# Narrower waits for reused memory, a later read of a guard flag, and a newly searched instruction order in a linear-attention and softmax-attention kernel

## The chip, the cores and the metric

The kernel runs on one core of one Trainium2 chip. The metric is device time in microseconds (us), the median of the fast runs. Every run told here was of the fast state. A profile gives the span from the first to the last instruction, which is 1.7 to 1.8 us shorter than the time of the same run.

Engines: PE is TensorE (PEld its weight loads), DVE is VectorE, ACT is ScalarE, POOL is GpSimd, SP is SyncE, which issues DMAs here.

## The reference

Two attention blocks over separate inputs of 2048 tokens, 512 features and 32 heads of 16, their outputs side by side. Block A is linear attention and is the smaller part. Block B is full softmax attention and bounds the kernel:

```python
scores = jnp.einsum("bhqd,bhkd->bhqk", q, k) * scale
p = _softmax(scores, axis=-1)
o = jnp.einsum("bhqk,bhkd->bhqd", p, v)
return (...o...).reshape(B, S, D) @ wo
```

## The kernel before

B's scores are cut into 2048 blocks of 128 keys by 512 queries. PE computes a block (QK) in PSUM, the memory that its matmuls write (`pS` in the profiles). Then one of two engines turns it into probabilities in an fp16 slot of 512 columns in the big tensor `MEM`:

- ACT, with a real exponential over two or three blocks at once (`128x1024`, `128x1536`);
- DVE, with one scale-and-add that builds the bits of an approximate exponential. POOL adds two shifted copies of it, so such a block needs three PV matmuls instead of one.

PE then multiplies the slot with V (PV). All other work (projections, block A, output matmuls) is interleaved.

A planner in the Python of the kernel decides the order. It simulates the engines with fixed durations and latencies, picks what goes next, and gives each engine a fixed in-order stream. Its choices are steered by `TABLE`, one row of eleven parameters per 20 us of planned time. The recording layer then works out the semaphore waits:

```python
def add(self, lane, fn, reads=(), writes=(), ...):
    for k in writes:
        if k in self.parts:
            writes = list(writes) + self.parts.pop(k)
    ...
    for r in writes:
        w = self.last_write.get(r)
        if w is not None: ... deps.add(w)
        for rd in self.readers.get(r, ()): deps.add(rd)
    ...
    for r in writes:
        self.last_write[r] = op
        self.readers[r] = []
```

`MEM` holds x (16 slots' worth) and the weights W (12 slots' worth) until the last projection; then those 28 slots open for blocks. `parts` tells which x or W keys lie under a slot:

```python
for i in range(P0):
    sch.parts[("PT", i)] = ([("xTb", t) for t in range(4 * (i % 4), 4 * (i % 4) + 4)] if i < W0 else
                            [("Wb", kd, g) for kd in range(2) for g in range(NGP)] + [("Wb", 2)])
```

The first writer of a slot thus becomes a writer of all the keys under it, and the first writer of the next slot with the same keys waits for it, though the two slots share no address.

The approximation holds for a limited range of scores, so a flag computed on the chip guards it. Every engine reads the flag into a register and, at its end, branches to a slow general path if it is too large. The read stands 200 recorded operations after the flag's own:

```python
def emit_queue(self, queue, eng, sems, dma_inc=16, hook=None):
    for op in self.queue_ops[queue]:
        for d in op.waits: ... eng.wait_ge(sems[d.lane], val)
        if hook is not None and op.idx > hook[0]:
            hook[1](eng)        # wait for the flag, load it
            hook = None
        ins = op.fn(eng)
...
    sch.emit_queue(queue, e, sems, hook=(flag_op.idx + 200, hook))
    with e.If(got[0] > THRESHOLD_BITS): ...general path...
```

## Time and profile before

| | before |
|---|---|
| time, first 3 runs | 696.84 us (693.53 to 696.85) |
| span of the profile | 693.2 us |
| busy: ACT, PE, DVE, POOL | 97%, 95%, 83%, 56% |
| ACT: exponentials of two and three blocks, block A's | 518, 127, 32 |

The view to trust is ACT's start-to-start intervals. Records of consecutive ACT instructions overlap, so gaps of a few tenths of a microsecond vanish inside the "busy" share. From here on, ACT's own work is 0.904 us per exponential of two blocks, 1.331 of three, 0.477 of one (the medians of those intervals in the trace, which the prediction rounded to 0.905, 1.33 and 0.48). Whatever an interval has beyond that is called a stall. Every span below is then head (to the first exponential) + work + stalls + tail (from the end of the last exponential).

### The profile page before, as it was taken

Reading aid. Unit: us, or ns where it says so; the run is one execution under the profiler, and the core shown is the slowest. Engines: PE = TensorE matmul, PEld = TensorE weight load, DVE = VectorE, ACT = ScalarE, POOL = GpSimd, SP = SyncE. Lnnn points to the kernel's source line nnn. Section 1 sums busy time; section 2 is a strip of 40 time slices with the busy share of each in tenths; the row PEclk is TensorE's granted clock in tenths of the full one; section 3 lists DMA queues with packets and bytes.
Section 4 is the critical chain, followed back from the end, with each engine's and each line's share of the span. In section 5 each row is a group of like instructions: output and inputs, shape, how many; then the busy total and the mean of one; then the engine's idle time right before and its main releaser. Section 6 shows DMA issues by size and latency. Waiting matters only on the chain.

```text
span 693.2 us, 16233 instructions
## 1 busy us (share of the span) xinstructions
PE 661.5 (95%) x6619; PEld 220.0 (32%) x6673; DVE 576.8 (83%) x952; ACT 669.0 (97%) x683; POOL 390.4 (56%) x666
## 2 busy tenths in 40 slices
PE   8999999999999999999999999999889999999997
PEld 5323333333433333233223222333222222222222
DVE  5988889778778978788889888787888988888893
ACT  5999999999999999999999999999999999999995
POOL 5667656434254755544466667334456775667672
PEclk9999999999999999999999999999999999999999
DMA  9910000000000000000200100001000011000001
GB/s 212 234 43 1 1 2 4 10 11 11 2 1 1 2 1 1 10 9 10 42 21 2 25 17 24 9 9 39 17 25 1 17 24 43 20 17 17 1 32 35
DMA packets 36576, 17.36 MB, mean 25 GB/s; under 512 B 27536, under 2 KB 35984, under 8 KB 36496
## 3 DMA queue, kind: packets, MB, share of 16 engines
q1 hardware_dynamic: 35408, 15.61, 9.5%
q8 instruction: 54, 0.88, 0.5%
q10 hardware_dynamic: 1088, 0.66, 0.4%
q14 instruction: 26, 0.21, 0.1%
HBM read 4.46 MB, written 4.19 MB: 12 GB/s over the span
## 4 chain that ended last, share of the span: by engine, by line
PE 41%; ACT 38%; DVE 17%; issue 2%; DMA 1%; POOL 0%; DVEq 0%; ACTq 0%; POOLq 0%
ACT MEM L1001 37%; PE pS L786 15%; PE pPV L1130 13%; DVE MEM L887 10%; PE pS L655 3%; PE pS L549 2%; PE pS L734 2%; PE pS L624 1%; ACT EA L646 1%; DVE OT L1154 1%; DVE OT L1162 1%; DMA MEM<-in_B_x_dram 1%; PE pPV L1352 1%; DVE VV L633 1%; PE pS L583 1%
## 5 line engine op out<-in xcount | busy, mean ns | idle before, releaser
L1001 ACT ACTIVATE MEM<-pS 128x1024 f16<-128x1024 f32 (+1 forms) x645 | 656.5, 1202 | 10.7 <-PE pS L786 7.9
L1076 POOL INT64_ADD MEM<-MEM x639 | 382.7, 612 | 289.3 <-DVE MEM L887 250.3
L887 DVE TENSOR_SCALAR MEM<-pS 128x512 int16<-128x512 f32 (+1 forms) x590 | 403.7, 720 | 76.5 <-PE pS L786 72.5
L786 PE MATMUL pS<-QT,KM 32*128 32x512 bf16 x2048 | 271.9, 385 | 15.8 <-ACT MEM L1001 8.1
L1130 PE MATMUL pPV<-MEM,VV 128*17 128x512 f16 x3310 | 284.6, 382 | 1.0 <-DVE OT L1154 0.6
L786 PEld LDWEIGHTS pS<-QT,KM 32*128 32x128 bf16 x2048 | 71.6, 91 | 244.6 <-ACT MEM L1001 186.5
L1130 PEld LDWEIGHTS pPV<-MEM,VV 128*17 128x17 bf16 x3310 | 60.9, 88 | 121.9 <-issue 97.2
L655 PE MATMUL pS<-Wa,xTa 128*128 128x256 bf16 x256 | 39.3, 275 | 0.2 <-DVE MEM L887 0.2
L549 PE MATMUL pS<-MEM 128*128 128x512 bf16 x98 | 29.5, 383 | 3.0 <-issue 1.2
L1154 DVE STREAM_TRANSPOSE OT<-pPV 128x512 f32<-128x512 f32 x32 | 22.6, 706 | 7.1 <-PE pPV L1130 7.1
L655 PEld LDWEIGHTS pS<-Wa,xTa 128*128 128x128 bf16 x256 | 19.7, 97 | 17.9 <-issue 9.3
L527 DVE CAST KNa<-pS 128x512 bf16<-128x512 f32 x30 | 20.5, 684 | 3.2 <-PE pS L734 1.9
L646 ACT ACTIVATE EA<-pS 128x512 bf16<-128x512 f32 x32 | 22.3, 696 | 0.0
L624 PE MATMUL pS<-MEM 128*128 128x128 bf16 x256 | 19.8, 220 | 1.0 <-DVE MEM L887 0.5
L1162 DVE TENSOR_TENSOR OT<-OT,ZR 128x256 bf16<-128x256 f32 x32 | 18.1, 566 | 0.9
L1352 PE MATMUL pPV<-ZW 128*17 128x256 bf16 x101 | 18.2, 274 | 0.0
L624 PEld LDWEIGHTS pS<-MEM 128*128 128x128 bf16 x256 | 14.5, 98 | 9.2 <-issue 5.1
L734 PE MATMUL pS<-WOa,KNa 128*128 128x512 bf16 x51 | 15.8, 383 | 1.7 <-DVE MEM L887 0.9
L681 PE MATMUL pS<-xTa,Wa 128*128 128x512 bf16 x52 | 15.8, 383 | 1.3 <-issue 1.0
L549 PEld LDWEIGHTS pS<-MEM 128*128 128x128 bf16 x120 | 8.7, 97 | 20.1 <-issue 10.1
L647 DVE TENSOR_SCALAR EA<-EA 128x512 bf16<-128x512 bf16 x32 | 12.8, 401 | 2.3 <-ACT EA L646 2.1
L629 DVE CAST VV<-pS 128x512 bf16<-128x512 f32 x16 | 11.0, 686 | 2.9 <-PE pS L624 2.8
(80 smaller groups left out, 225.3 us busy)
## 6 DMA issues: line engine op xcount, KB each, us to landing
out_dram<-KNa SPq DMA_DIRECT2D x30, 128.0 KB, 1.7
Wa<-in_A_wqkv_dram SPq DMA_DIRECT2D x1, 1536.0 KB, 7.6
KM<-KR SPq DMA_DIRECT2D x96, 16.0 KB, 1.8
MEM<-in_B_wqkv_dram SPq DMA_DIRECT2D x2, 384.0 KB, 6.2
MEM<-in_B_wqkv_dram SPq DMA_DIRECT2D x1, 512.0 KB, 4.4
WOb<-in_B_wo_dram SPq DMA_DIRECT2D x1, 512.0 KB, 8.5
WOa<-in_A_wo_dram SPq DMA_DIRECT2D x1, 512.0 KB, 9.2
MEM<-in_B_x_dram ACTq DMA_DIRECT2D x1, 256.0 KB, 2.9
```

Of the source, the lines that this page charges most:

```text
L549: return e.matmul(f32v(bk), lhsT=Wb[:, cc, kind * 512 + Gp * 128:kind * 512 + Gp * 128 + 128], rhs=xTb[:, cc, sc * 512:(sc + 1) * 512], st ...
L624: return e.matmul(f32v(bk)[:, tl * 128:(tl + 1) * 128], lhsT=xTb[:, cc, t * 128:(t + 1) * 128], rhs=Wb[:, cc, 1024 + Gp * 128:1024 + Gp * ...
L646: ("act", 0.06 + n * 0.000833, f_ev("act", lambda e, bk: e.activation(EA[:, q, 0:n], f32v(bk)[:, c0:c0 + n], ACTF.Exp), [], [("EA", q)])),
L655: return e.matmul(f32v(bk)[:, 256 * tt:256 * tt + 256], lhsT=xTa[:, cc, (t2 + tt) * 128:(t2 + tt + 1) * 128], rhs=Wa[:, cc, 512 * kind + 2 ...
L734: return e.matmul(f32v(bk), lhsT=src, rhs=WO[:, hb, :], start=(hb == 0), stop=(hb == 3))
L786: return e.matmul(dst, lhsT=KM[32 * g:32 * g + 32, Gp % 2, e_, j * 128:(j + 1) * 128], rhs=QT[32 * g:32 * g + 32, Gp % 2, c * 512:(c + 1) ...
L887: sch.add("dve", lambda e: e.tensor_scalar(PTi[:, i * 512:(i + n) * 512], PS[:, b0 * 512:(b0 + n) * 512], ESC, EB, op0=ALU.mult, op1=ALU.add),
L1001: sch.add("act", lambda e: e.activation(PT[:, p0 * 512:p0 * 512 + w], PS[:, use[0] * 512:use[0] * 512 + w], ACTF.Exp, scale=SC), reads=[(" ...
L1076: sch.add("pool", lambda e: e.int64_add(PTl[:, pos * 128:pos * 128 + w], PTl[:, p0 * 128:p0 * 128 + w], v_), reads=[("PT", p0 + i) for i i ...
L1130: sch.add("pe", lambda e, g=g, j=j, hl=hl, pi=pi, k=k, first=first, last_=last_: e.matmul(PVb[32 * g:32 * g + 17, 0:512], lhsT=VV[:, Gp % ...
L1154: sch.add("dve", lambda e: e.transpose(OT[:, 0, :], PVb[:, 0:512]), reads=[("PV", g) for g in range(4)], writes=[("OT", 0)])
L1352: ins = e.matmul(dst, lhsT=ZW[:, 0:17], rhs=ZW[:], start=first, stop=first, tile_position=(0, 32 * g))
```

## The change

Three parts. A slot's first writer waits only for readers and writer of the memory under it and no longer becomes that memory's writer. The flag is read after everything else on each engine. And the order is new: `TABLE` comes from a beam search (a search that keeps only the best few tables at each step), and the planner counts 0.11 us between dependent DVE instructions (0 before) and 6.3 us instead of 5.0 for spreading K by DMA.

```diff
     def add(self, lane, fn, reads=(), writes=(), name="", queue=None,
             extra_deps=(), accum=None, force_signal=False):
-        for k in writes:
-            if k in self.parts:
-                writes = list(writes) + self.parts.pop(k)
...
+        for k in writes:
+            for r in self.parts.pop(k, ()):
+                deps.update(self.readers.get(r, ()))
+                if r in self.last_write:
+                    deps.add(self.last_write[r])
         for r in writes:
             w = self.last_write.get(r)
...
     TABLE = [      # 36 rows before, 33 after; almost all differ
-        (3, 0.05, 0.6, 1.0, 6, 9, 2, 0.8, 0.5, 4.0, 4),
+        (3, 0.1, 1.0, 0, 16, 8, 2, 0.8, 0, 4.0, 4),
...
-               ("dve", "dve"): 0.0, ("dve", "dma"): 0.12, ...
+               ("dve", "dve"): 0.11, ("dve", "dma"): 0.12, ...
...
-            st.append(("dma", 5.0, spread))
+            st.append(("dma", 6.3, spread))
...
-                              bank=False, ready=t_, prio=0.5))
+                              bank=False, ready=t_ + LAT["dve", "dve"], prio=0.5))
...
-            sch.emit_queue(queue, e, sems, hook=(flag_op.idx + 200, hook))
+            sch.emit_queue(queue, e, sems, hook=(len(sch.ops), hook))
```

## The prediction

> **What bounds the kernel now.** I read the busy shares first, then the chain that ended last, then ACT's own groups and its timeline.
>
> ```profile
> PE 661.5 (95%) x6619; PEld 220.0 (32%) x6673; DVE 576.8 (83%) x952; ACT 669.0 (97%) x683; POOL 390.4 (56%) x666
> ...
> PE 41%; ACT 38%; DVE 17%; issue 2%; DMA 1%; POOL 0%; DVEq 0%; ACTq 0%; POOLq 0%
> ```
>
> ACT is busy 669.0 of 693.2 us. The chain passes back and forth between ACT and PE, so these two wait for each other closely; PE's 95% says less, because matmul ends are modelled. Next, what one ACT instruction takes out of ACT's time. Mean durations (1119 and 1541 ns) overlap, so I take start to next start from the timeline (start, length, instruction, count):
>
> ```profile
> 505.14 9.27 ACT L1001 ACTIVATE MEM<-pS 128x1024 f16<-128x1024 f32 x10 [1.45 <-POOL MEM L1076]
> 514.20 0.70 ACT L646 ACTIVATE EA<-pS 128x512 bf16<-128x512 f32 x1
> 514.68 8.47 ACT L1001 ACTIVATE MEM<-pS 128x1024 f16<-128x1024 f32 x9
> ```
>
> Ten exponentials of two blocks run from 505.14 to 514.20: 0.905 us each. The one of 512 columns takes 514.68 - 514.20 = 0.48. So 512 columns cost 0.425, and three blocks 0.905 + 0.425 = 1.33 us. The counts come from the groups by shape:
>
> ```profile
> L1001 ACT ACTIVATE MEM<-pS 128x1024 f16<-128x1024 f32 x518 | 505.8, 1119 | 6.5 <-PE pS L786 3.9 <-POOL MEM L1076 1.8
> ...
> L1001 ACT ACTIVATE MEM<-pS 128x1536 f16<-128x1536 f32 x127 | 193.0, 1541 | 4.2 <-PE pS L786 4.0
> ...
> L646 ACT ACTIVATE EA<-pS 128x512 bf16<-128x512 f32 x32 | 22.3, 696 | 0.0
> ```
>
> ACT's unavoidable work is 518 x 0.905 + 127 x 1.33 + 32 x 0.48 = 468.8 + 168.9 + 15.4 = 653.1 us. The first exponential starts at 10.48 and the last ends at 684.20 (682.53 + 1.67 in the chain), 673.7 us apart. So 20.6 us of ACT's time between them are stalls, most of them hidden in the "busy" figure because each is shorter than the overlap of two records. Before lie 10.5 us of head, after it 9.0 us of tail (last PV, transposes, output matmuls, store). Head 10.5 + work 653.1 + stalls 20.6 + tail 9.0 = 693.2.
>
> Where are the stalls? I subtracted 0.905, 1.33 or 0.48 from every start-to-start interval on ACT. Two places stand out as the change's targets. The first is the moment when the memory of x and W opens for block slots:
>
> ```profile
> 497.38 1.99 ACT L1001 ACTIVATE MEM<-pS 128x1024 f16<-128x1024 f32 x2
> 500.17 2.14 ACT L1001 ACTIVATE MEM<-pS 128x1024 f16<-128x1024 f32 x2 [0.80 <-PE pS L786]
> 502.67 1.02 ACT L1001 ACTIVATE MEM<-pS 128x1024 f16<-128x1024 f32 x1 [0.36 <-POOL MEM L1076]
> 505.14 2.85 ACT L1001 ACTIVATE MEM<-pS 128x1024 f16<-128x1024 f32 x3 [1.45 <-POOL MEM L1076]
> ```
>
> Five exponentials took 505.14 - 497.38 = 7.76 us instead of 4.53: 3.2 us lost, and the releaser is POOL, which never otherwise holds ACT. The second is the read of the guard's flag in mid-stream:
>
> ```profile
> 283.81 1.02 ACT L1001 ACTIVATE MEM<-pS 128x1024 f16<-128x1024 f32 x1
> 285.86 2.36 ACT L1001 ACTIVATE MEM<-pS 128x1536 f16<-128x1536 f32 x2 [1.03 <-PE pS L786]
> ```
>
> 2.05 - 0.905 = 1.1 us lost. The sequencer records there show a register load of 0.47 us on ACT at 285.21, one of 0.49 on PE at 284.27, 0.54 on DVE and 0.50 on POOL, each followed by an ALU step and an assertion, 0.65 to 0.76 us per engine in all. One more stall of 1.7 us ends at 27.70 (early projections). The remaining 14.6 us are some fifty gaps of 0.1 to 0.9 us, nearly all released by the QK matmuls of PE.
>
> **What the Trainium skill says.** "ScalarE: Activation LUTs", section "What ACT_TABLE_LOAD costs", gives 0.833 ns per column for any function, and 186 ns less a 93 ns overlap as the fixed part. The slope agrees (0.425 us per 512 columns is 0.830 ns); the fixed part here is 0.905 - 0.853 = 0.05 us, so I use the trace. "DMA: Bandwidth & Descriptors", section "Latency and other measured facts", puts the floor of a register load at about 600 ns; here 0.47 to 0.54. "Runtime: NRT & Kernel Launch", section "Instruction fetch mechanics", says that a taken branch out of the fetched window stalls for a fetch. That seems to set the end here: ACT's closing branch at 689.76 is followed by its drain at 692.87, 3.1 us later, while POOL had seen the last store at 691.74.
>
> **The change part by part.**
>
> *Slot waits.* Before, the first writer of each of the 28 slots became a writer of all the x or W keys under it. The 12 slots of W therefore wait for one another in a single chain, the 16 of x in four chains, across ACT, DVE and POOL, though their addresses differ. After it, each waits only for readers (old projections, long done). This should remove the 3.2 us. I count 2.7: a little of the stall at 500.17 ended with PE and may be there anyway.
>
> *Flag read.* It leaves the middle: -1.1 on ACT. It is added at each engine's end, where ACT's path (last store issue, load, branch, fetch, drain) sets the finish: +0.7. POOL's read also comes after its wait for the last store: 691.74 + 0.76 plus its drain, still ahead of ACT's. Net -0.4.
>
> *Order.* This is the large part, and only the instruction counts are known:
> - exponentials of two blocks 518 to 534, of three 127 to 110: 19 blocks of 2048 move from ACT to DVE. ACT: 16 x 0.905 - 17 x 1.33 = 14.5 - 22.6 = -8.1 us.
> - DVE: 512-wide block instructions 549 to 594, 1024-wide 41 to 28. Start to start they take 0.60 and 1.13 in the trace: 45 x 0.60 - 13 x 1.13 = +12.3 us. DVE's busy time becomes 589, some 86% of the new span.
> - POOL: pairs of shifted copies 623 to 646, singles 16 to 8: 23 x 0.60 - 8 x 0.40 = +10.6 us, 59% of the span. No bound.
> - PE: 38 more PV matmuls, but 50 fewer zero filler matmuls (139 to 89; about 0.11 us apart in the trace, 5.5 us). With each run of matmuls priced at the quick end of what the same run took before, PE's stream sums to 634 us before and 629 after, an estimate. PE gets no heavier.
>
> The planner's added 0.11 us for a dependent DVE step and 6.3 instead of 5.0 us for the K copies cost nothing themselves; they make the plan's order more honest.
>
> Sum on ACT: -8.1 - 2.7 - 0.4 = -11.2. With the 16 us of other stalls taken as unchanged, the span goes from 693.2 to 682.0. Another -0.5 is a guess for fewer planned gaps: the fall in fillers says that the plan leaves PE idle less often. So 681.5 for the span, 11.7 less. From the median of 696.84 that gives 685.1; I say 685.0.
>
> **Rivals.**
> 1. *PE becomes the bound and gives ACT's gain back as stalls.* For it: most small stalls of ACT already end with QK. PE has 693.2 - 634 = 59 us not needed, and would keep 681.5 - 629 = 52; utilisation between the ends rises only from about 94% to 95%. If a third of the 8.1 comes back as QK-released gaps, the span is 684 and the time 688. I think this the likeliest way to miss.
> 2. *DVE becomes the bound.* In stretches without projections it is busy about 19 of 20 us already. More DVE blocks there would delay the freeing of the PSUM banks in which PE places the next blocks, so PE and then ACT wait. Against it: DVE was idle 116 us, mostly in stretches with other work. If half the added 12.3 us were exposed, there would be nearly no gain: 691.
> 3. *The opening wait is replaced.* Slots now free at once, but PV must still drain the POOL copies; if that is what limits, ACT loses the same 3 us slightly later: 688.
> 4. *The search also removes unplanned stalls.* If the 16 us fall by 5: 680.
>
> **Range and chances.** The arithmetic of -8.1 is firm, the 3.8 of removed waits nearly so; the uncertainty is how much of the residual 16 us grows or shrinks, to me a standard error of about 4.5 us, and the spread of the three times before (693.5 to 696.9) adds about 1. Range 678.5 to 691. Faster by over 2% means under 682.9, 2.1 us below my centre: 0.33. Slower by over 2% needs a blunder of 25 us: 0.01. The rest, 0.66.
>
> **What would show it.** ACT's count must be 534 and 110 and its stall total about 16 us instead of 20.6. Around the opening (after some 1490 of 2048 QK blocks) no interval on ACT may be released by POOL; if one is, the slot part is wrong. No register load stands in mid-stream; the interval from ACT's last store to its drain should grow from 3.1 to about 3.8 us. If ACT's intervals released by QK sum to well over 16 us, rival 1 or 2 holds; DVE's share of the releases of PE's weight loads tells which. The prediction would be badly wrong if the tail after the last exponential grew beyond 10 us, or if new waits on the K copies appeared on PE.

## The result, and the profile after

The changed kernel took 675.47 us (674.94 to 677.03, 4 runs), the kernel before 695.18 us (693.12 to 696.85, 4 runs): a ratio of 0.9722, 95% interval 0.9683 to 0.976. Ratios here are the mean time of one kernel's fast runs over that of the other's of the same rounds, so not quite the ratio of the quoted medians. The forecast of 685.0 with a range of 678.5 to 691.0 was too slow.

The page of the changed kernel, its busy shares and the chain that ended last:

```profile
PE 644.0 (96%) x6606; PEld 211.1 (31%) x6661; DVE 583.7 (87%) x984; ACT 658.1 (98%) x682; POOL 401.4 (60%) x681
...
ACT 74%; PE 17%; DVE 5%; issue 1%; DMA 1%; POOL 1%; ACTq 0%; DVEq 0%
```

The chain had lain on PE for 41% and on ACT for 38%. Now it runs along ACT for 74% of the span: ACT is seldom made to wait. Its groups by shape (busy us, mean ns, idle before):

```profile
L1000 ACT ACTIVATE MEM<-pS 128x1024 f16<-128x1024 f32 x534 | 520.2, 1172 | 0.7 <-PE pS L785 0.4
...
L1000 ACT ACTIVATE MEM<-pS 128x1536 f16<-128x1536 f32 x110 | 171.1, 1580 | 1.0 <-PE pS L785 1.0
```

The counts are those forecast. Visible idle time before them fell from 6.5 + 4.2 to 0.7 + 1.0 us. The mean duration of a two-block exponential rose from 1119 to 1172 ns although the work is the same. That is a good sign here: start to start they stay 0.904 us apart, and an exponential that had to wait has a shorter record (1.02 us in the single rows further below), so a longer mean says that fewer had to wait.

Where the 19.6 us between the two profiles come from:

| us | span | head | ACT work | stalls | tail |
|---|---|---|---|---|---|
| before | 693.2 | 10.5 | 652.6 | 21.1 | 9.0 |
| after | 673.6 | 8.8 | 644.4 | 10.7 | 9.7 |
| difference | -19.6 | -1.7 | -8.2 | -10.4 | +0.7 |
| predicted | -11.7 | 0 | -8.1 | -4.3 | +0.7 |

Work and tail came as forecast. The stalls fell 6.1 us further, and the head was 1.7 us shorter, which nobody had forecast.

The head can be settled from the traces. PE's first 20 projection matmuls, before and after (start, length):

```profile
6.33 3.57 PE L1232 MATMUL pS<-MEM 128*128 128x128 bf16 x20 [0.97 <-DMA MEM<-in_B_x_dram]
```

```profile
6.49 1.92 PE L1231 MATMUL pS<-MEM 128*128 128x128 bf16 x20 [1.53 <-DMA MEM<-in_B_x_dram]
```

The same matmuls take 3.57 or 1.92 us, and nothing in the change touches them. Either the change does this by some roundabout way, or the pace varies from run to run. The runs below decide.

### The profile page after: what moved, and what is told of

It reads as the page before. It is cut to its first block, busy times and chain, and to the rows that moved or that the text cites. A ratio compares the mean times of both kernels' runs of the same rounds, so it can differ in the third digit from the quotient of the medians.

```text
span 673.6 us, 16251 instructions
## 1 busy us (share of the span) xinstructions
PE 644.0 (96%) x6606; PEld 211.1 (31%) x6661; DVE 583.7 (87%) x984; ACT 658.1 (98%) x682; POOL 401.4 (60%) x681
## 4 chain that ended last, share of the span: by engine, by line
ACT 74%; PE 17%; DVE 5%; issue 1%; DMA 1%; POOL 1%; ACTq 0%; DVEq 0%
ACT MEM L1000 72%; PE pPV L1129 7%; PE pS L785 6%; DVE MEM L886 3%; ACT EA L645 2%; PE pS L548 1%; DMA MEM<-in_B_x_dram 1%; PE pS L654 1%; POOL MEM L1075 1%; DVE EA L646 1%; PE pS L680 0%; PE pS L1181 0%; DVE OT L1161 0%; DVE OT L1153 0%; PE pS L592 0%
## 5 line engine op out<-in xcount | busy, mean ns | idle before, releaser
L1000 ACT ACTIVATE MEM<-pS 128x1024 f16<-128x1024 f32 (+1 forms) x644 | 646.6, 1242 | 1.7 <-PE pS L785 1.4
L1075 POOL INT64_ADD MEM<-MEM x654 | 393.7, 615 | 258.2 <-DVE MEM L886 229.7
L886 DVE TENSOR_SCALAR MEM<-pS 128x512 int16<-128x512 f32 (+1 forms) x622 | 416.1, 706 | 53.1 <-PE pS L785 49.5
L1129 PE MATMUL pPV<-MEM,VV 128*17 128x512 f16 x3348 | 279.7, 382 | 0.6 <-DVE ZR L1160 0.3
L785 PE MATMUL pS<-QT,KM 32*128 32x512 bf16 x2048 | 264.1, 384 | 13.6 <-ACT MEM L1000 7.9
L785 PEld LDWEIGHTS pS<-QT,KM 32*128 32x128 bf16 x2048 | 68.9, 91 | 244.5 <-ACT MEM L1000 202.9
L1351 PE MATMUL pPV<-ZW 128*17 128x256 bf16 x75 | 14.5, 274 | 0.0
L548 PEld LDWEIGHTS pS<-MEM 128*128 128x128 bf16 x120 | 8.2, 97 | 18.5 <-issue 10.1
L733 PE MATMUL pS<-WOb,MEM 128*128 128x512 bf16 x40 | 12.4, 384 | 0.6 <-issue 0.6
```

The lines of the kernel that those rows point to most:

```text
L548: return e.matmul(f32v(bk), lhsT=Wb[:, cc, kind * 512 + Gp * 128:kind * 512 + Gp * 128 + 128], rhs=xTb[:, cc, sc * 512:(sc + 1) * 512], st ...
L733: return e.matmul(f32v(bk), lhsT=src, rhs=WO[:, hb, :], start=(hb == 0), stop=(hb == 3))
L785: return e.matmul(dst, lhsT=KM[32 * g:32 * g + 32, Gp % 2, e_, j * 128:(j + 1) * 128], rhs=QT[32 * g:32 * g + 32, Gp % 2, c * 512:(c + 1) ...
L886: sch.add("dve", lambda e: e.tensor_scalar(PTi[:, i * 512:(i + n) * 512], PS[:, b0 * 512:(b0 + n) * 512], ESC, EB, op0=ALU.mult, op1=ALU.add),
L1000: sch.add("act", lambda e: e.activation(PT[:, p0 * 512:p0 * 512 + w], PS[:, use[0] * 512:use[0] * 512 + w], ACTF.Exp, scale=SC), reads=[(" ...
L1075: sch.add("pool", lambda e: e.int64_add(PTl[:, pos * 128:pos * 128 + w], PTl[:, p0 * 128:p0 * 128 + w], v_), reads=[("PT", p0 + i) for i i ...
```

## The experiments

There were twelve runs. The first eight take the parts apart: each of the three alone, each pair, the kernel before again, and the old table with the new latencies. All instruction orders come from the two plans except where said. The new table with the old latencies could not be run: in simulation the order that it gives reads PSUM in the middle of an accumulation. So "the order" below is always the new table and the new latencies together.

In the table "stalls" are ACT's, worked out as above from each run's own profile.

| run | time | ratio to before | span | head | work | stalls | tail |
|---|---|---|---|---|---|---|---|
| before again | 696.13 | 0.9992 | 695.0 | 8.4 | 652.6 | 25.0 | 9.1 |
| slots | 690.66 | 0.9927 | 688.7 | 8.8 | 652.6 | 18.3 | 9.0 |
| flag | 697.21 | 1.0017 | 694.2 | 8.5 | 652.6 | 23.0 | 10.2 |
| slots + flag | 690.94 | 0.9939 | 689.2 | 8.6 | 652.6 | 17.8 | 10.2 |
| order | 679.15 | 0.9755 | 676.3 | 8.4 | 644.4 | 13.5 | 9.9 |
| order + slots | 674.55 | 0.9703 | 673.1 | 8.5 | 644.4 | 11.4 | 8.9 |
| order + flag | 678.05 | 0.9753 | 677.0 | 8.3 | 644.4 | 14.2 | 10.2 |
| all three, again | 675.07 | 0.9693 | 673.1 | 8.3 | 644.4 | 10.7 | 9.7 |
| old table, new latencies | 700.09 | 1.0071 | 697.5 | 8.5 | 666.9 | 11.9 | 10.2 |

### Before again: the head

No edit.

> The kernel before, once more, for the head: theory H says that the first 20 projection matmuls of PE take either about 1.9 or about 3.6 us from run to run in one and the same program (before's profile had the slow ones, after's the fast ones), so the 1.7 us of the head are no effect of the change. If they take 3.6 us again here and 1.9 in the three kernels with a changed part, something in the program causes it.

```profile
6.08 1.92 PE L1232 MATMUL pS<-MEM 128*128 128x128 bf16 x20 [1.36 <-DMA MEM<-in_B_x_dram]
```

The unchanged kernel now has the fast matmuls and a head of 8.4 us. So the 1.7 us are no effect of the change. A later run with the new order, the one with the rearranged end, had 3.57 us again. "TensorE: Matmul & The Clock Gate" of the Trainium skill, section "What's actually happening", describes a clock gate that halves the clock until PE has been busy for a window of some 3.4 us, and that window runs freely, so where it falls varies from run to run. A factor of 1.86 between 3.57 and 1.92 fits it, and the traces' own clock records agree: the first record of full clock starts at 10.47 and 9.69 us in the two profiles with the slow matmuls, and between 3.9 and 6.4 us in the other twelve (`--windows` shows 1.00 for the time ahead of that record).

The repeat brought a surprise as well. Its stalls are 25.0 us instead of 21.1, all of the difference in one place.

### The slot rule alone

```diff
 # before, with the change's rule in add(): nothing else
+        for k in writes:
+            for r in self.parts.pop(k, ()):
+                deps.update(self.readers.get(r, ())) ...
```

> Slot rule only, in the old order and with the old flag read. The program's instructions stay in the same order; only waits go. Theory S: 2.5 to 3.5 us off (about 692 us), the interval at the opening shrinks from 7.8 to about 5 us for five exponentials, no release by POOL there, and the small gaps elsewhere stay about 16 us. Theory K: 6 us or more off, with smaller gaps all through the last 190 us.

The result is 5.1 us by the ratio (0.9927, interval 0.9908 to 0.9946), between the two theories. At the opening ACT's stalls over 0.3 us are all gone in this run (none from 492 to 592 us), and with them the release by POOL. The opening in the repeat of the kernel before, on ACT's timeline:

```profile
498.10 2.14 ACT L1001 ACTIVATE MEM<-pS 128x1024 f16<-128x1024 f32 x2 [0.80 <-PE pS L786]
500.60 1.02 ACT L1001 ACTIVATE MEM<-pS 128x1024 f16<-128x1024 f32 x1 [0.36 <-POOL MEM L1076]
503.07 4.69 ACT L1001 ACTIVATE MEM<-pS 128x1024 f16<-128x1024 f32 x5 [1.45 <-POOL MEM L1076]
508.56 1.02 ACT L1001 ACTIVATE MEM<-pS 128x1024 f16<-128x1024 f32 x1 [0.80 <-PE pS L786]
510.18 2.10 ACT L1001 ACTIVATE MEM<-pS 128x1024 f16<-128x1024 f32 x2 [0.60 <-PE pS L786]
512.74 1.02 ACT L1001 ACTIVATE MEM<-pS 128x1024 f16<-128x1024 f32 x1 [0.47 <-PE pS L786]
514.36 1.02 ACT L1001 ACTIVATE MEM<-pS 128x1024 f16<-128x1024 f32 x1 [0.59 <-PE pS L786]
```

The first three rows are the waits seen in the first profile, to within 0.01 us. The four after them are new: PE is late, four times, for 0.5 to 1.0 us. The stretches of the same runs tell why. The columns after the length are the busy times of PE, PEld, DVE, ACT and POOL, then PE's granted clock. First the repeat of before, then the run with the slot rule:

```profile
490.00:505.00 15.00, 11.80 (x130) 3.68 (x129) 11.19 (x18) 12.14 (x13) 8.45 (x14) 1.00 0.11 27
505.00:512.00 7.00, 6.90 (x35) 1.32 (x32) 4.02 (x6) 5.55 (x7) 2.39 (x4) 0.55 0.15 37
512.00:516.00 4.00, 3.53 (x14) 0.80 (x14) 2.48 (x5) 2.57 (x4) 1.20 (x2) 0.51 0.00 0
```

```profile
490.00:505.00 15.00, 14.42 (x153) 4.87 (x155) 12.92 (x20) 14.83 (x16) 9.61 (x16) 1.00 0.11 27
505.00:512.00 7.00, 6.75 (x71) 1.95 (x68) 6.78 (x13) 7.00 (x10) 3.52 (x6) 1.00 0.15 37
512.00:516.00 4.00, 4.00 (x56) 0.89 (x48) 4.00 (x8) 4.00 (x6) 3.10 (x7) 1.00 0.02 4
```

In the repeat PE pauses behind the slot waits, and then its clock is granted at half (0.55, 0.51 in these stretches; by the trace's clock records from 505.65 to 515.89 us). PE gets through 35 matmuls in seven microseconds instead of 71. In the first profile of the kernel before, the same stretch had a clock of 1.00 and no such stalls. So the slot waits cost 3.2 us in each of the three profiles with the old order and the old rule, and more where the clock falls behind them: 3.5 us in the repeat, 2.4 in the run with the flag alone, nothing in the first profile. The skill's page, in the same section, has the clock fall to a half after at least one idle window of about 3.4 us. The half agrees; the idling does not. In the 3.41 us before the fall PE was busy for 1.87 us, and its longest pause was 1.54 us. A pause of 1.55 us stands in the first profile too, with no fall behind it. What decides between the two, no run shows.

The run-to-run spread carries the same mark. Over the 90 fast runs of the kernel before whose clock is on record, time and mean granted clock correlate at -0.88: 14 runs at a clock of 0.998 or more have a mean of 693.5 us, 19 runs from 0.990 to under 0.993 one of 698.0. The 16 runs with the slot rule average a clock of 0.9987 and a median of 690.66. They are not wholly free of it: two of them, at 0.995, took 694.5 and 695.4 us.

Theory K had the wrong reach (nothing lasts to the end of the kernel) but the right kind: a wait can have a sequel, through the clock and not through the order of streams.

### The flag alone

```diff
-            sch.emit_queue(queue, e, sems, hook=(flag_op.idx + 200, hook))
+            sch.emit_queue(queue, e, sems, hook=(len(sch.ops), hook))
```

> Flag read at each engine's end only, old order, old slot rule. Theory S: -1.1 in mid-stream, +0.7 at the end, so within 0.1% of before. Theory K: 2 us or more off, since the gaps of 0.9 us some 13 us after the old flag read and others like it go as well.

The ratio is 1.0017 (0.9995 to 1.004): nothing, or a little worse. ACT's stall at the old place fell from 1.14 to 0.49 us and not to zero. The gap of 0.95 us thirteen microseconds later stayed, so it was no sequel of the flag. The tail grew from 9.1 to 10.2 us, more than the 0.7 forecast. The load and its checks take 0.6 us on ACT as expected, and besides the last store's issue on ACT took 1.34 us instead of 0.37 to 0.41. In every profile with the flag at the end it took 0.92 to 1.40 us; why, no run shows.

### The order alone, and the pairs

```diff
 # the change's TABLE, the three LAT, spread and ready lines; old add(), old hook
```

> New order only: the new table and planner latencies; the old rule for block slots and the old mid-stream flag read stay. Theory S (sum of independent parts): the order alone carries most of the gain, time 679 to 682 us, ACT stalls after the first exponential about 14 to 15 us (10.7 as in the full change, plus about 3 at the opening of the slots and about 1 at the flag). Theory K (knock-on: in-order engines stay out of step long after a wrongly placed wait, so waits and order multiply): 684 us or more, and ACT's small gaps after the opening are larger than in the full change.

Measured 679.15 us with stalls of 13.5 us: theory S. The opening is cheaper in this order. It costs 0.68, 0.36 and 1.16 us on ACT, 2.2 in all, with a release by POOL again.

> The full change without the flag part: new order, new slot rule, flag still read in mid-stream (at another place of the new order). Theory S (independent parts; flag worth nothing): within 0.1% of the full change, about 675 to 676 us; ACT stalls about 11.3 us with one near the flag read of some 0.6 us, tail 9.0 instead of 9.7 us.

> The full change without the slot part. In the order-only run the opening cost 2.2 us on ACT, in the old order 3.2 to 6.7. If the slot rule's worth depends on the order, this should be 677 to 679 us, 2 to 3 us above the full change and not 5; if it were worth the same 5 us in every order, 680 us or more.

> Both wait parts in the old order: slots alone gave -5 us and the flag alone 0 to +1, so 690 to 692 us, ACT stalls about 17.5 us. The distance from here to the full change is then the order alone with clean waits: -8.2 of ACT work and about -7 of stalls, 15 us. In particular the gaps near 25.7 (1.7 us), 174 (0.6), 296 (0.95) and 401 (0.7) must still be there, as in every run of the old order, if they belong to the order; if they came from the old waits or the flag they are gone.

Order + slots took 674.55 us, against 675.47 and 675.07 for all three: the flag part gains nothing and may cost up to 1 us. Order + flag took 678.05, 2.6 to 3.0 us over all three, as expected. But its profile has a stretch at half clock too, from 381.46 to 384.87 us, far from the opening and with no pause of PE over 0.34 us in the 3.41 us before; it cost ACT 1.26 us. The other pair, order against order + slots, gives 4.6 us (3.6 by the ratios to before). So the slot rule's worth in the new order lies between 2.6 and 4.6 us; that it is less than the 5.1 of the old order rests on the stalls at the opening (2.2 against 3.2 us), not on the times. Slots + flag took 690.94 us: with clean waits the order alone is worth 690.94 - 675.47 = 15.5 us, of which 8.2 is ACT work and 17.8 - 10.7 = 7.1 are stalls.

Those 7.1 us are most of what the prediction missed, and the traces show what they were. In slots + flag, near 25.8 us, on ACT:

```profile
19.48 4.78 ACT L1003 ACTIVATE MEM<-pS 128x1024 f16<-128x1024 f32 x5
25.83 4.69 ACT L1003 ACTIVATE MEM<-pS 128x1024 f16<-128x1024 f32 x5 [1.57 <-PE pS L788]
```

The same stretch in the full change:

```profile
19.54 11.58 ACT L1000 ACTIVATE MEM<-pS 128x1024 f16<-128x1024 f32 x11
```

The stall of 1.69 us stands at this place in every profile of the old order (1.60 to 1.69 us), whatever was done to the waits, and in none of the new one. The same holds for those near 174 (0.62), 296 (0.95), 343 (0.37) and 401 us (0.69): from run to run they repeat to 0.1 us. They belong to the order. Sorted by size, the whole difference lies in such gaps: those over 0.3 us sum to 8.0 us (13 gaps) in slots + flag and to 0.9 us (2 gaps) in the full change, all smaller ones to 9.5 and 9.4 us.

The planner's own account of its order, which it writes to the list `TRACE`, when one is given, as the program is built, says where most of them come from. Matched one to one with ACT's instructions, it has 4.8 us of gaps on ACT in the old order, at just these places (1.06 before the exponential at 25.8 us, 0.63, 0.85, 0.36, 0.50) and at the flag's (0.51 near 283), and 0.0 us in the new one. On the chip the old order's planned gaps over 0.1 us came to 5.5 us in slots + flag. So the search had removed gaps that the old plan contained, and the chip followed. Stalls that no plan contained changed little: 17.8 - 5.5 = 12.3 us with the old order, 10.7 with the new. Among them, seven lone gaps of 0.3 to 0.7 us (3.2 us together; the largest, 0.68, near 213 us) went with the old order as well, though its plan has none there. Six of the seven stand in every profile of that order. Why, no run shows.

### The old table with the new latencies

```diff
 # the full change, with the old TABLE
```

> The full change with the old table: an order planned with the new latencies but a table that was never searched for them. The planner's own account has ACT ending 25 us later than with the new table (13 us later than the old pair) and about 6 us of planned gaps. Theory P (what the search does to the plan passes to the chip one to one): about 700 us, 24 to 27 us above the full change. Theory L (the corrected latencies themselves make the order run better on the chip than planned): 3 us or more below that, with ACT's unplanned stalls under 8 us instead of 10 to 11.

It took 700.09 us. The plan passes to the chip: the planner had ACT end 25.4 us later than in the full change, and the time is 24.6 to 25 us longer. Of these, 22.5 us are more ACT work (666.9 against 644.4), so the run tests the count of exponentials more than the gaps. My count of its planned gaps was wrong (2.5 us, not 6); at their six places the chip has 2.6 us. Stalls are 11.9 us, so 9.3 are unplanned. That is above the 8 that theory L asked for, but below the 10.7 of the full change and the 12.3 of the old latencies. A small part for the corrected latencies, one or two microseconds, is possible. This order also has a less busy DVE (80%), so the run does not separate the two.

### The flag read ahead of the waits

Why did the read in mid-stream cost ACT 0.6 us at all? In the old emission the hook came after the waits of the next operation. The built program shows that these waits then sit on the load: on ACT the load waited for the same matmuls as the exponential behind it, and only then began its 0.65 us.

```diff
         for op in self.queue_ops[queue]:
+            if hook is not None and op.idx > hook[0]:
+                hook[1](eng)
+                hook = None
             for d in op.waits:
                 ...
-            if hook is not None and op.idx > hook[0]:
-                hook[1](eng)
-                hook = None
             ins = op.fn(eng)
 # and hook=(flag_op.idx + 200, hook) as before; new order, new slot rule
```

> New order, new slot rule, the flag read in mid-stream at the same instruction as in the run with the flag part undone, but the register load now stands ahead of that instruction's own waits instead of behind them. Theory W (the read cost ACT 0.6 us because the load had to wait for the same matmuls as the exponential behind it, and then delayed that exponential): the gap of 0.63 us near 224 us falls under 0.1 us, ACT stalls 10.4 to 10.8 us, tail about 8.9 us, span near 672.5. Theory D (the load occupies ACT's sequencer for 0.65 us wherever it stands and ACT starves): a gap of 0.5 us or more stays.

The place of the read in order + slots, then in this run:

```profile
219.41 3.86 ACT L1000 ACTIVATE MEM<-pS 128x1024 f16<-128x1024 f32 x4
223.65 2.86 ACT L1000 ACTIVATE MEM<-pS 128x1024 f16<-128x1024 f32 x3 [0.38 <-PE pPV L1129]
```

```profile
218.59 7.51 ACT L1000 ACTIVATE MEM<-pS 128x1024 f16<-128x1024 f32 x8
```

The break of 0.63 us is gone, with no price in the tail (8.6 us). Span 672.3, time 674.53 us (ratio 0.9709, 0.9678 to 0.9739). Theory W holds: the load itself is hidden under the running exponential; it was only in the wrong place relative to a wait. The gain over the full change, near 1 us, shows in the profile, but the intervals of the times do not separate the two.

### The end rearranged

```diff
+            back = {"act": 2, "dve": 6, "pool": 1}.get(queue)
+            at = sch.queue_ops[queue][-back].idx if back else len(sch.ops)
-            sch.emit_queue(queue, e, sems, hook=(len(sch.ops), hook))
+            sch.emit_queue(queue, e, sems, hook=(at, hook))
 # hook ahead of the waits as above; the four last stores all issued by SP
```

> The full change with its end rearranged: ACT, DVE and POOL read the flag while they wait for the last matmuls or stores, ahead of those waits, and all four last stores are issued by SP, so that ACT's closing branch follows its last copy at once. If ACT's chain (last store issue, register load, branch, fetch, drain) sets the end, the tail after the last exponential falls from 9.7 to 8.0 to 8.6 us and the time to about 674 us, 1 to 1.5 us under the full change. If the landing of the last store on POOL sets it instead, the tail stays over 9 us.

The tail fell to 8.5 us, so ACT's closing chain did set the end. The run changes the place of the read and the issuer of the stores together; the tail of 8.6 us in the run before, where only the read had left the end, says that the read is nearly all of it. Now POOL's drain at 673.42 comes after ACT's at 672.30: the landing of the last store sets it. The profiled run had the slow matmuls in its head (10.1 us), so its span of 673.7 hides the gain. The time, 675.43 us (ratio 0.9711), is not to be told from that of the full change.

### A version that beats both

```diff
 # the end rearranged, and a TABLE from a second beam search over the same planner:
```

> The changed kernel once more, beside the next run, as its yardstick on the same chip: 675 to 676 us, ACT stalls 10.7 us and the same gaps near 91 and 131 us to within 0.05 us, since stalls have repeated from run to run for one and the same order. The head differs by 0 or about 1.6 us, whichever pace PE's first 20 projection matmuls take.

> Try at a version that beats both: the rearranged end of the run before, and a table from another beam search over the same planner. By counts ACT has 549 exponentials of two blocks and 97 of three, 3.7 us less work than in the full change; the planner's own account leaves about 3 us of that as gaps. Theory P (work and planned gaps pass to the chip one to one): 2 us less than the full change, about 673.5 us, ACT stalls 13 to 14 us. If unplanned stalls grow because DVE and PE are fuller (rival 1 or 2 of the prediction): 676 us or more, stalls over 16 us.

The repeat of the full change held to what was expected: stalls 10.7 us, gaps of 0.50 and 0.42 us near 90 and 131 us, head 8.3 us. Beside each other on one chip: 675.07 us (674.80 to 675.63) for the full change and 672.63 us (672.12 to 674.31) for this version, 6 runs each; ratios to before 0.9693 (0.9666 to 0.9721) and 0.9659 (0.9631 to 0.9688). These intervals overlap, but the runs of the two do not. Its page:

```profile
PE 643.9 (96%) x6642; PEld 210.7 (31%) x6696; DVE 588.3 (88%) x986; ACT 654.6 (98%) x684; POOL 407.9 (61%) x692
```

The bill: work 640.7 us (3.7 less), stalls 12.7 (2.0 more), tail 8.4 (1.3 less). The planner's account has 2.8 us of gaps in it, near 411, 474, 602 and 618 us. The chip has stalls of 0.67, 0.33, 0.86 and 0.82 us at these four exponentials. Theory P again, with stalls a little under the 13 to 14 us expected. With DVE at 88% the unplanned stalls did not grow.

## Why the prediction was wrong

The steps, one by one:

- **ACT's work, -8.1.** Right: -8.2. Counts times intervals of the trace before is a sum that held here.
- **Slot waits, -2.7.** Right in mechanism and too small. In the profile at hand the opening cost 3.2 us; over all runs the slot rule is worth 5.1 us in the old order. The rest fits the half clock after the opening, which that one profile did not have.
- **Flag, -0.4 net.** Wrong in sign by the profiles; the times do not settle it. Mid-stream it gave -0.65, since 0.49 of the 1.14 us was a planned gap. At the end it cost 0.7 to 1.2 us of tail in most pairs of runs (0.2 in one). From ACT's last store to its drain the profiles have 3.54 us before and 4.25 after, +0.7 as forecast; the prediction's 3.1 counts from the branch. Moving the read ahead of a wait was the better cure.
- **"With the 16 us of other stalls taken as unchanged", and "-0.5 is a guess for fewer planned gaps".** This is the step that failed. Of those stalls, about 5.0 us were gaps that the old plan itself contained (5.5 with the one at the flag), and the search had taken all of them out. With clean waits, stalls fell 7.1 us between the orders, where the prediction had 0.5. The planner could have told: its accounts of the old order and of the new have ACT end at 672.2 and 659.7 us, and gaps of 4.8 and 0.0 us. The prediction took the counts alone from the new program.
- **Head.** The prediction left it alone, rightly; the profile before happened to have the slow one, so 1.7 of the 19.6 us between the two profiles is chance.
- **The base, 696.84.** The sums come from the profile of a run of 695.0 us, but the forecast takes them off a median that is 1.8 us higher. So the miss of 9.5 us is 6.1 of stalls, 1.7 of head and 1.8 of base. The stalls alone would have brought the forecast to 678.9.
- **Rival 1 (PE takes the gain back) and rival 2 (DVE does).** Neither. PE's share went to 96%, DVE's to 87%, and ACT's stalls halved. Rival 1, called "the likeliest way to miss", had no term in the centre, but with rival 2 it stretched the range upward, to 691.
- **Rival 3 (the opening wait is replaced).** No. In the full change no interval on ACT is released by POOL, and none near the opening exceeds 0.3 us.
- **Rival 4 (the search also removes stalls).** This is what happened, with 6 to 7 us instead of 5; but the prediction called those stalls unplanned, and most of what went was planned.

The stalls could have been sorted from the first trace. The prediction has "some fifty gaps of 0.1 to 0.9 us" for the last 14.6 us. The trace has 47 such gaps outside the three named places, 11.4 us in all, the rest being smaller still; and ten of them, over 0.3 us and lone, hold 5.2 of the 11.4. With the 1.7 us near 27.7, which the prediction also left in place, these were what the new order did not inherit. What stays open: how much the corrected latencies gave by themselves, and why the last store's issue on ACT takes two to four times as long when the flag is read at the end.

## What to carry to other kernels

Split the idle time of the bounding engine by origin before carrying it over to a changed schedule: gaps that the order itself contains vanish or appear with the order (5.5 us here), while the small ones stayed (9.5 and 9.4 us). A false wait in front of TensorE can cost about twice its length when the granted clock drops behind it (3.2 and 3.5 us here), so read the clock of the stretch after it and look at more than one run. And a register load was free ahead of the next instruction's wait and cost ACT 0.63 us behind it.

## What the Trainium skill lacked or had wrong

- "ScalarE: Activation LUTs", section "What ACT_TABLE_LOAD costs": the slope of 0.833 ns per column holds, but back-to-back exponentials from PSUM with immediate scale have a fixed part of 0.05 us (0.477, 0.904 and 1.331 us for 512, 1024 and 1536 columns), not the 0.09 that 186 ns less an overlap of 93 ns gives.
- "DMA: Bandwidth & Descriptors", section "Latency and other measured facts": the floor of about 600 ns for a register load is high; loads of one word took 0.46 to 0.55 us here, in all but two cases on DVE (0.81 and 0.83).
- "TensorE: Matmul & The Clock Gate", section "What's actually happening": the half clock and the window agree (three stretches at half clock, in three profiles, lasted 3.41, 6.83 and 10.24 us, one, two and three times 3.41). But its table has the clock fall after at least one idle window of about 3.4 us. Here it fell with PE busy for 95% and more of the span, after windows of 3.41 us in which PE was busy for 46% to 83% and never paused for more than 1.55 us. The run-to-run spread goes with them (693.5 us at a granted clock of 0.998 or more, 698.0 at 0.990 to under 0.993).
- "Runtime: NRT & Kernel Launch", section "Instruction fetch mechanics": it gives no figure for the stall of a taken branch. From the start of ACT's closing branch to its drain it was 2.65 to 3.2 us in most profiles, and up to 4.1. That this is the fetch is the page's reading; no run here shows it.
- No page has that a wait emitted ahead of a register load is carried by the load: 0.63 us on ACT, gone when the load stood ahead of the wait.
- No page has that the issue of a store on ACT took 0.92 to 1.40 us instead of 0.36 to 0.41 when the engines read a register at their end.
